# Attention with a mixture of experts: row numbering, routing compares and weight splitting placed on GpSimd, V splitting and softmax denominators placed elsewhere

## The chip, the cores and the metric

The kernel runs on one core of a Trainium2 chip. A core has TensorE (PE in the profile, with its weight loads as PEld), VectorE (DVE), ScalarE (ACT), GpSimd (POOL) and SyncE (SP), each with its own instruction queue that is worked off in order, and DMA queues that SP and POOL feed. The metric is the time of one execution in device microseconds; lower is better. Three executions of the kernel before took 776.6, 773.53 and 778.3 us, so the median is 776.6 us.

## The reference

First attention, then a mixture of experts on its output. Every one of 8 batches and 8 heads has 512 local and 32 global tokens with head dimension 64.

```
s_g  = scale * q_g @ [k_g, k_l]^T          # 32 global queries see everything
out_g = softmax(s_g) @ [v_g, v_l]
s_ll = where(|i - j| <= 32, scale * q_l @ k_l^T, -1e9)
out_l = softmax([scale * q_l @ k_g^T, s_ll]) @ [v_g, v_l]
# softmax: e = exp(s - max); e / (sum(e) + 1e-09)
x = concat([out_g, out_l]) as (4352, 512)

logits = x @ w_gate                        # 8 experts
e_idx  = argmax(logits);  gate_w = softmax(logits)[e_idx]
eom    = sigmoid(x @ w_output_gate)
out[rows of e] = gate_w * eom[e] * (relu(x @ w1[e]) @ w2[e])   # w1 512x1024, w2 1024x512
```

All in float32. Routing is by data: which rows go to which expert is known only when the logits are.

## The kernel before, in words

**Attention.** Per batch there are ten units of work: eight `Local` units (a pair of heads and half of the four 128-query blocks) and two `Global` units (32 queries of four heads each). The list `us` holds four locals, a global, two locals, a global, two locals. `advance(u)` (line 591) makes one step of a pipeline over these units; in step k TensorE computes the scores of unit k (`scores`, into one of two `sp` banks), transposes the probabilities of unit k-2 (`tF`, `tD`, into two `pt` banks), and multiplies unit k-3 with V (`pv`, into one of two `po` banks). In the same step DVE takes the row maximum of unit k (`mx`; for half of the locals, the fused ones, the mask is added in it) and splits the transposed probabilities of unit k-2 into a low half (`loF`, `loD`, lines 309 and 317), each behind the high half that ACT makes (`hiF`, `hiD`, lines 305 and 313); then it normalizes the unit that `pv` finished in the step before: denominators (`den`, L287: sum plus a small constant, times a factor), reciprocal (`rec`, L291), product (`norm`, L340). ACT also makes the exponentials (`ex`, L278). Products run in split float16 or bfloat16, a high and a low half each.

**V.** The V of a batch comes as five float32 tiles `vf` (`load_v`, L131), which `split_v` turns into a float16 half (a copy) and a bfloat16 rest (a subtraction), both on GpSimd; `gp` records each GpSimd call under L83 and keeps their written order. `copy_v` (L141, L142) then copies parts of both halves to other partitions by DMA. For batch 0 all this is written ahead of the first unit, and SP issues the copies ahead of the small constants `ids`, `crt` (L176) and `wrf`.

**Routing.** A `Router` holds four or five tiles of 128 rows (two or three in the last batches). `split` (L439) halves a tile, a DMA transposes it, TensorE makes 16 logits per row. Then `small` gives a list of tiny steps, about twenty, which `fill` slips between the DVE instructions of the attention steps of the next batch: argmax, softmax, a rank of each row among the rows of its expert (`rank`), then `m_fin` (L545: writes the gate into eight columns of each tile, then SP writes the tiles to DRAM, L548) and `m_row` (L538: one 128x128 compare-and-multiply per tile, which marks the place of each row and puts the row's number there). All of these are on DVE. The row numbers `rowf` and a few constants are made by thirteen DVE instructions (L185 to L207) from `crt`; they stand ahead of the first unit's `mx` in DVE's queue. When six batches are routed, `list_pre` (L714) compares the tiles with three early lists (`at_pre`, L717, one DVE instruction) and TensorE gathers the rows of expert 0 that are worked ahead of the others.

**Expert 0's first weights** are loaded in batch 2 (`w1r`, 2 MB). ACT scales and rounds an eighth of them at two places in each of batches 3 to 6 (`ahead1`); the eight low halves (`w1l`, L83) are subtracted on GpSimd in the last batch.

**Order.** The order on PE, DVE, ACT and SP is that in which the program is written (`manual_schedule`); GpSimd's `gp` calls keep theirs too. After attention, at about 340 us, comes the list of all rows and then 36 slots of 128 gathered rows through the experts, which this change does not touch.

Of the kernel before, what the change touches and what calls it, by code (L numbers as in the profile page):

```python
# [10 lines left out]
F32 = mybir.dt.float32  # L11
# [47 lines left out]
def tile_attention_moe(  # L59
# [79 lines left out]
    def copy_v(b):  # L139
        for t in sets[b % 2][0:2]:  # L140
            nc.sync.dma_start(t[0:64, 5:8], t[64:128, 0:3])  # L141
            nc.sync.dma_start(t[64:96, 5:8], t[64:96, 4:5].broadcast_to([32, 3, VW]))  # L142
# [42 lines left out]
    nc.vector.tensor_scalar(rowf, c_k, c_s, 2.0, op0=ALU.add, op1=ALU.add)  # L185
    for n, views in ((4, (rowf[:, 0:16], rowf[:, 17:25])), (2, (rowf[:, 25:33],))):
        far = const.tile([P, 1], F32, name=f"far{n}")
        nc.vector.tensor_scalar(far, c_s, 1.0, n - 1.0, op0=ALU.add, op1=ALU.mult)
        step = const.tile([P, n], F32, name=f"step{n}")
        nc.vector.scalar_tensor_tensor(step, c_k[:, 0:n], -(P - 1.0) / P, far.broadcast_to([P, n]), ALU.mult, ALU.add)  # L190
        for v in views:
            v = v.rearrange("p (b i) -> p b i", i=n)
            nc.vector.tensor_tensor(out=v, in0=v, in1=step.unsqueeze(1).broadcast_to(list(v.shape)), op=ALU.add)
    for r in range(1, 3):
        nc.vector.tensor_scalar(rowf[:, PART[r]:PART[r + 1]], rowf[:, PART[r]:PART[r + 1]], -float(PART[r] * P), None,
                                op0=ALU.add)
# [6 lines left out]
    nc.vector.tensor_copy(count, count_i)  # L203
    slot = const.tile([P, NSLOT + 1], F32, name="slot")
    nc.vector.tensor_scalar(slot, count_i[:, 0:NSLOT + 1], -1.0, None, op0=ALU.add)
    slot_at = const.tile([P, NSLOT + 1], F32, name="slot_at")
    nc.vector.tensor_scalar(slot_at, slot, float(KPRE), float(P), op0=ALU.add, op1=ALU.mult)  # L207

    tile_at = const.tile([P, NT], F32, name="tile_at")
    row_at = const.tile([P, NT, P], F16, name="row_at")  # L210

# [4 lines left out]

    ohsum = const.tile([P, 8], BF16, name="ohsum")
# [373 lines left out]
    def advance(u):  # L591
# [585 lines left out]
```

## Time and profile before

| | us |
|---|---|
| median of three runs | 776.6 |
| the profiled execution's own time | 778.0 |
| its span, first to last instruction | 776.1 |
| PE busy | 692.7 (89%) |
| DVE busy | 399.3 (51%) |
| ACT busy | 362.0 (47%) |
| POOL busy | 211.8 (27%) |
| one batch of attention in the steady part, units 7 to 7 | 34.8 |
| first 20 us: PE busy | 4.5 |

Shares over the whole span say little here, because the program has two parts. Up to about 340 us, attention and routing, PE, DVE and ACT are all busy most of the time; after that the experts run on PE nearly alone. What is asked of a stage has to be read from windows of that stage, and from the chain of waits inside it. Two reading aids: the time of an instruction in the profile includes some overlap with its neighbour on the same engine, so steps are better taken from one start to the next; and a wait for several semaphores is shown under the one that came last.

### The profile page before, as it was taken

To read this page: it belongs to the slowest core of one execution; us is meant where nothing else is said; L and a number is where in the kernel's file an instruction comes from. 1 tells how busy PE (TensorE), PEld (TensorE's weight loads), DVE (VectorE), ACT (ScalarE), POOL (GpSimd) and SP (SyncE) were. 2 spreads that over 40 slices of the span, in tenths; PEclk is the share of its full clock that TensorE was granted. 3 is DMA by queue.
4 is the path that set the end of the run, shared out by engine and by line. 5 is a ranking of instruction groups with operands and counts; after the bars stand their busy time and mean duration, and the time that the engine had idled before them with its cause. 6 is when DMAs were issued, how large, how long until landed. Compare 5 with 4: busy or idle time off the path is not lost.

```text
span 776.1 us, 23116 instructions
## 1 busy us (share of the span) xinstructions
PE 692.7 (89%) x9042; PEld 528.7 (68%) x9042; DVE 399.3 (51%) x1261; ACT 362.0 (47%) x781; POOL 211.8 (27%) x266
## 2 busy tenths in 40 slices
PE   2699999999899987976899989999999978999991
PEld 1588878778676866846677767777776747777760
DVE  0689899898979897770324301133133333332200
ACT  0578777878768787310333411133235151433210
POOL 6333443527241747131011221212221211121110
PEclk9999999999989998997999999999999999999997
DMA  7628696677938466439267594253864959654110
GB/s 225 211 44 240 175 273 185 163 240 144 301 64 272 73 193 140 99 104 314 48 194 248 100 179 104 79 171 78 199 191 142 184 170 189 157 109 89 47 35 21
DMA packets 113604, 120.17 MB, mean 155 GB/s; under 512 B 81551, under 2 KB 83215, under 8 KB 111570
## 3 DMA queue, kind: packets, MB, share of 16 engines
q1 hardware_dynamic: 106706, 96.85, 49.3%
q0 software_dynamic: 6528, 19.67, 8.9%
q14 instruction: 295, 2.42, 1.2%
q8 instruction: 75, 1.23, 0.7%
HBM read 200.50 MB, written 19.42 MB: 283 GB/s over the span
## 4 chain that ended last, share of the span: by engine, by line
issue 45%; PE 19%; DVE 18%; POOL 10%; DMA 2%; ACT 1%; SPq 1%; POOLq 1%; DVEq 0%; ACTq 0%
POOL out_dram L674 5%; POOL qkv L1020 4%; PE sp L249 4%; DVE fl L309 3%; DVE dl L317 3%; DVE p L265 2%; DVE nm L260 2%; PE pt L296 2%; DMA vf<-in_vD_dram 2%; PE pt L301 2%; PE sp L659 1%; DVE row_at L538 1%; POOL qkv L83 1%; PE sp L358 1%; PE pt L387 1%
## 5 line engine op out<-in xcount | busy, mean ns | idle before, releaser
L659 PE MATMUL ph<-qkv,w1h 128*128 128x128 f16 x2304 | 203.7, 222 | 17.4 <-DMA qkv<-qkv 9.8
L659 PEld LDWEIGHTS <-w1h 128*128 128x128 f16 x2496 | 196.9, 100 | 26.7 <-issue 10.5
L659 PE MATMUL ph<-qkv,w1l 128*128 128x128 f16 x1152 | 200.7, 222 | 9.1 <-DVE w1l L686 6.1
L670 PE MATMUL py<-qkv 128*128 128x512 f16 x864 | 192.0, 379 | 0.0
L666 DVE SCALAR_TENSOR_TENSOR qkv<-ph,qkv 128x512 f16<-128x512 f32 x72 | 46.7, 687 | 207.3 <-ACT qkv L665 103.0
L670 PEld LDWEIGHTS <-qkv 128*128 128x128 f16 x896 | 86.0, 98 | 97.0
L659 PEld LDWEIGHTS <-w1l 128*128 128x128 f16 x1248 | 124.2, 100 | 10.3 <-DVE w1l L686 6.4
L665 ACT ACTIVATE qkv<-ph 128x512 f16<-128x512 f32 x72 | 39.8, 594 | 162.4 <-PE ph L659 81.3
L674 POOL DMA_INDIRECT out_dram<-qkv x36 | 36.3, 1008 | 207.6 <-ACT qkv L673 207.0
L249 PE MATMUL sp<-qkv 64*128 64x224 f32 x512 | 69.0, 390 | 20.8 <-DVE nb L265 13.7
L83 POOL TENSOR_TENSOR xr<-xt,xr 128x512 f16<-128x512 f32 x30 | 34.7, 1158 | 152.3 <-ACT xr L439 88.3
L1020 POOL DMA_INDIRECT qkv<-xd,idx x36 | 35.8, 995 | 138.6 <-DMA out_dram<-qkv 135.1
L249 PEld LDWEIGHTS sp<-qkv 64*128 64x128 f32 x512 | 45.7, 194 | 25.0 <-DVE nb L265 14.1
L278 ACT ACTIVATE p<-p,nb 128x224 f32<-128x224 f32 x128 | 51.0, 473 | 24.6 <-DVE nb L265 24.3
L686 DVE SCALAR_TENSOR_TENSOR w1l<-w1r,w1h 128x512 f16<-128x512 f32 x56 | 34.4, 685 | 42.8 <-ACT w1h L684 30.5
L317 DVE SCALAR_TENSOR_TENSOR dl<-pt,dh 128x512 f16<-128x512 f32 x80 | 53.4, 667 | 0.6 <-ACT dh L313 0.2
L690 ACT ACTIVATE qkv<-qkv 128x512 f16<-128x512 f32 x56 | 33.7, 627 | 42.7 <-PE py L670 30.5
L305 ACT ACTIVATE fh<-pt 96x512 f16<-96x512 f32 x64 | 37.7, 589 | 32.9 <-PE pt L296 29.4
L673 ACT ACTIVATE qkv<-py,qkv 128x512 f32<-128x512 f32 x36 | 24.8, 688 | 58.3 <-PE py L670 34.0
L692 DVE SCALAR_TENSOR_TENSOR qkv<-qkv 128x512 f16<-128x512 f32 x56 | 34.5, 686 | 33.3 <-ACT qkv L690 33.3
L313 ACT ACTIVATE dh<-pt 128x512 f16<-128x512 f32 x80 | 47.1, 589 | 8.1 <-PE pt L387 6.0
L328 PE MATMUL po<-qkv,fh 96*128 96x65 f16 x256 | 48.2, 196 | 2.7 <-DVE lg L454 2.7
(189 smaller groups left out, 1473.3 us busy)
## 6 DMA issues: line engine op xcount, KB each, us to landing
w1r<-in_w_dram SPq DMA_DIRECT2D x38, 2048.0 KB
qkv<-in_w_dram SPq DMA_DIRECT2D x38, 2048.0 KB
vf<-in_vD_dram SPq DMA_DIRECT2D x40, 260.0 KB
qkv<-in_kT_dram SPq DMA_DIRECT2D x7, 1280.0 KB
qkv<-in_qT_dram SPq DMA_DIRECT2D x7, 1088.0 KB
xd<-xr SPq DMA_DIRECT2D x6, 1056.0 KB
qkv<-qkv SPq DMA_DIRECT2D x16, 195.0 KB
xd<-xr SPq DMA_DIRECT2D x4, 528.0 KB
```

Source lines behind the costliest of these rows:

```text
L83: i = tc.keep_in_program_order(getattr(nc.gpsimd, name)(*args, **kw))
L249: nc.tensor.matmul(self.sp[:, 2 * hd + bi, 0:W], lhsT=self.q[hs, pr, qs], rhs=self.k[hs, pr, ks], start=(bi == 0 or self.fused), stop=self ...
L278: nc.scalar.activation(self.p[:, n], src, AF.Exp, bias=self.nb[:, n:n + 1], scale=sc)
L313: nc.scalar.mul(self.dh, self.pD, PS)
L317: nc.vector.scalar_tensor_tensor(self.dl, self.pD, PS, self.dh, ALU.mult, ALU.subtract)
L328: nc.tensor.matmul(o, lhsT=fh, rhs=self.vh[0:96, 4 + i, hc], start=True, stop=False)
L659: nc.tensor.matmul(o, lhsT=w[:, k], rhs=xT[:, x], start=(n == 0), stop=(n == 11))
L665: nc.scalar.activation(hh[:, gs], v, AF.Relu)
L666: nc.vector.scalar_tensor_tensor(hl[:, gs], v, 0.0, hh[:, gs], ALU.max, ALU.subtract)
L670: nc.tensor.matmul(py, lhsT=h[:, f], rhs=w, start=(f == 0 and n == 0), stop=(f == 7 and n == 2))
L674: i = nc.gpsimd.indirect_dma_start(out=out[:, :], out_offset=bass.IndirectOffsetOnAxis(ap=x[:, XG:XG + 1].bitcast(U32), axis=0), in_=y, in ...
L1020: nc.gpsimd.indirect_dma_start(out=xs, out_offset=None, in_=xd[:, :], in_offset=bass.IndirectOffsetOnAxis(ap=idx[:, s + 1:s + 2], axis=0))
```

## The change

1. **V of batch 0.** `split_v(0, i)` makes the high half on ACT and the low half on DVE, and is called after the second unit (tiles 0, 4, 1) and after the third (tiles 2, 3). `copy_v` is called in two parts there. The third and fourth head pairs' Q and K are loaded ahead of V's tiles 2 and 3. Batches 1 to 7 keep GpSimd. The load of batch 1's Q and K moves from the first to the third unit of batch 0.
2. **Row numbering.** The thirteen instructions become `number()` on GpSimd, called in the fourth unit of batch 0.
3. **Denominators.** `den` becomes one ACT instruction (`Identity` with a scale and a bias tile `tiny`), and is issued before `mx` in `advance`.
4. **Routing compares.** `m_row` and `m_fin` run on GpSimd, except for the last group.
5. **Early list.** `at_pre` is made by three GpSimd instructions in a step of its own, `list_at`, ahead of `close`; `list_pre` waits at least one step after it.
6. **Expert 0's low halves** are subtracted in batches 4 to 7, two in each.

```diff
 def split_v(b, i):
     vh, vl, _, _ = sets[b % 2]
-    gp.tensor_copy(vh[:, i], raw[i])
-    gp.tensor_sub(vl[:, i], raw[i], vh[:, i])
+    if b == 0:
+        nc.scalar.copy(vh[:, i], raw[i])
+        nc.vector.tensor_sub(vl[:, i], raw[i], vh[:, i])
+    else:
+        gp.tensor_copy(vh[:, i], raw[i])
+        gp.tensor_sub(vl[:, i], raw[i], vh[:, i])
...
-    for i in (0, 4, 1, 2, 3):
+    for i in (0, 4, 1):
         load_v(0, i)
     load_pairs(0, 2, 4)
-    for i in (0, 4, 1, 2, 3):
-        split_v(0, i)
-    copy_v(0)
+    for i in (2, 3):
+        load_v(0, i)
...
-    nc.vector.tensor_scalar(rowf, c_k, c_s, 2.0, op0=ALU.add, op1=ALU.add)
...
+    def number():
+        gp.tensor_scalar(rowf, c_k, c_s, 2.0, op0=ALU.add, op1=ALU.add)
...
 def den(self):
     self.dn = wk.tile([P, 4], F32, name="dn", bufs=4)[self.ps]
-    nc.vector.tensor_scalar(self.dn, self.heads()[:, :, D], PS * 1e-9, 1 / XS, op0=ALU.add, op1=ALU.mult)
+    nc.scalar.activation(self.dn, self.heads()[:, :, D], AF.Identity, bias=tiny[self.ps], scale=1 / XS)
...
 def m_row(t):
     n = self.t0 + t
-    ts(row_at[:, n], count, st["md"][:, t:t + 1], rowf[:, n:n + 1], op0=ALU.is_equal, op1=ALU.mult)
+    (ts if last else gp.tensor_scalar)(row_at[:, n], count, st["md"][:, t:t + 1], rowf[:, n:n + 1], ...)
...
 def m_fin():
     for t in range(T):
-        ts(self.tiles[t][2][:, DM:XG], st["s3"][:, t:t + 1].broadcast_to([P, XG - DM]), YSC, None,
+        (ts if last else gp.tensor_scalar)(self.tiles[t][2][:, DM:XG], ...
...
 # advance
     d = ended.pop(0) if ended else None
+    if d:
+        d[0].den()
     if a:
         a.mx()
         fills(0)
         a.mb()
     if d:
-        d[0].den()
         fills(1)
...
+def list_at():
+    for t in range(KPRE):
+        gp.tensor_scalar(at_pre[:, :, t], tile_at[:, 0:NPRE], float(t * P), None, op0=ALU.is_equal)
+    listed.append(step[0] + 1)
...
 # loop over batches and units
-            if n == 0 and b + 1 < B:
+            if n == (0 if b else 2) and b + 1 < B:
                 load_pairs(b + 1, 0, 4)
...
+            if b == 0 and n in (1, 2):
+                for i in ((0, 4, 1), (2, 3))[n - 1]:
+                    split_v(0, i)
+                copy_v(0, n - 1, 2 * n - 1)
...
+            if b == 0 and n == 3:
+                number()
...
+            if b >= B - 4 and n in (1, 3):
+                f = 2 * (b + 4 - B) + n // 2
+                gp.tensor_sub(w1l[f], w1r[:, :, f * P:(f + 1) * P], w1h[f])
...
-                if n < 8:
-                    gp.tensor_sub(w1l[n], w1r[:, :, n * P:(n + 1) * P], w1h[n])
```

What this does to the order of instructions shows at three places. (The changed file's lines are numbered seven to twenty higher: L131 keeps its number, the copies L141 and L142 become L145 and L146, `mx` L260 and L265 become L267 and L272, `den` L287 becomes L294, the constant `crt` L176 becomes L179.) PE's instructions keep their order throughout.

The first place is SP's queue at the start, from the load of V on. Before:

```order
L131 DMA vf<-in_vD_dram 128x520 x5
L124 DMA qkv<-in_qT_dram 128x1088
L125 DMA qkv<-in_kT_dram 128x2x640
L141 DMA qkv<-qkv 64x1560
L142 DMA qkv<-qkv 32x3x520
```

The changed kernel, at the same place:

```order
L131 DMA vf<-in_vD_dram 128x520 x3
L124 DMA qkv<-in_qT_dram 128x1088
L125 DMA qkv<-in_kT_dram 128x2x640
L131 DMA vf<-in_vD_dram 128x520 x2
L175 DMA ids<-in_c_ids_dram 128x34
L179 DMA crt<-in_c_rt_dram 128x118
L218 DMA wrf<-in_wr_dram 128x4x16
L236 DMA xd<-w1r 1x528
L145 DMA qkv<-qkv 64x520
L146 DMA qkv<-qkv 32x520
```

The copies, which need split V, now stand behind the constants and no longer ahead of them. Before, the rows of `ids` and `crt` follow the copies.

The second place is DVE's queue at the start. Before, the rows between the cast of `identb` and the first `mx` (shown as ISA with its accumulator `nb`) are the numbering; its first two and last three of thirteen:

```order
L152 CAST identb<-ident 128x128
L185 TENSOR_SCALAR rowf<-crt 128x34
L188 TENSOR_SCALAR far_151<-crt 128x1
...
L203 CAST count<-count_i 128x128
L205 TENSOR_SCALAR slot<-count_i 128x42
L207 TENSOR_SCALAR slot_at<-slot 128x42
L265 ISA p,nb<-sp,mask 128x224
```

The changed kernel, at the same place, with the rows up to the first maximum of the fourth unit:

```order
L156 CAST identb<-ident 128x128
L272 ISA p,nb<-sp,mask 128x224
L272 ISA nb 128x1
...
L267 TENSOR_REDUCE nm<-sp 128x4
L138 TENSOR_TENSOR qkv<-vf,qkv 128x520 x3
L267 TENSOR_REDUCE nm<-sp 128x4
L316 SCALAR_TENSOR_TENSOR fl<-pt,fh 96x512
L324 SCALAR_TENSOR_TENSOR dl<-pt,dh 128x512
L138 TENSOR_TENSOR qkv<-vf,qkv 128x520 x2
```

The numbering is gone from the front, and five subtractions of V stand between the first units' work.

The third place is a step in the middle of attention, on ACT and on GpSimd. ACT's rows around the first global unit's exponential (`pgbuf`), before:

```order
L305 ACTIVATE fh<-pt 96x512
L313 ACTIVATE dh<-pt 128x512
L374 ACTIVATE pgbuf_135<-sp,nb 128x544
L305 ACTIVATE fh<-pt 96x512
L313 ACTIVATE dh<-pt 128x512
```

The same rows of the changed kernel:

```order
L312 ACTIVATE fh<-pt 96x512
L320 ACTIVATE dh<-pt 128x512
L294 ACTIVATE dn<-po,tiny 128x4
L381 ACTIVATE pgbuf_121<-sp,nb 128x544
L312 ACTIVATE fh<-pt 96x512
```

A `dn` stands behind each `dh` now, ahead of the exponentials of the step. On GpSimd the rows where a group of four tiles is finished and the next group's split begins, in the changed kernel:

```order
L83 TENSOR_TENSOR qkv<-vf,qkv 128x520
L83 TENSOR_SCALAR xr<-s_1905 128x8 x4
L83 TENSOR_TENSOR xr<-xt,xr 128x512
L83 COPY xr<-ids 128x8
L83 TENSOR_SCALAR row_at<-count,md,rowf 128x128 x4
```

Before, the two rows of TENSOR_SCALAR aren't there, and the rows of `xr` follow the last of V directly.

More of the change, by code (lines that the diff above doesn't have):

```diff
@@ L184, in tile_attention_moe @@
     rowf = const.tile([P, NT], F32, name="rowf")
[L185 to L196, printed above, removed]
     part = const.tile([P, 3], F32, name="part")
@@ L202, in tile_attention_moe @@
     count = const.tile([P, P], BF16, name="count")
-    nc.vector.tensor_copy(count, count_i)
     slot = const.tile([P, NSLOT + 1], F32, name="slot")
-    nc.vector.tensor_scalar(slot, count_i[:, 0:NSLOT + 1], -1.0, None, op0=ALU.add)
     slot_at = const.tile([P, NSLOT + 1], F32, name="slot_at")
-    nc.vector.tensor_scalar(slot_at, slot, float(KPRE), float(P), op0=ALU.add, op1=ALU.mult)
     tile_at = const.tile([P, NT], F32, name="tile_at")
     row_at = const.tile([P, NT, P], F16, name="row_at")
+    def number():
+        gp.tensor_scalar(rowf, c_k, c_s, 2.0, op0=ALU.add, op1=ALU.add)
+        for n, views in ((4, (rowf[:, 0:16], rowf[:, 17:25])), (2, (rowf[:, 25:33],))):
+            far = const.tile([P, 1], F32, name=f"far{n}")
+            gp.tensor_scalar(far, c_s, 1.0, n - 1.0, op0=ALU.add, op1=ALU.mult)
+            step = const.tile([P, n], F32, name=f"step{n}")
+            gp.tensor_scalar(step, c_k[:, 0:n], -(P - 1.0) / P, far, op0=ALU.mult, op1=ALU.add)
+            for v in views:
+                v = v.rearrange("p (b i) -> p b i", i=n)
+                gp.tensor_tensor(out=v, in0=v, in1=step.unsqueeze(1).broadcast_to(list(v.shape)), op=ALU.add)
+        for r in range(1, 3):
+            gp.tensor_scalar(rowf[:, PART[r]:PART[r + 1]], rowf[:, PART[r]:PART[r + 1]], -float(PART[r] * P), None,
+                                    op0=ALU.add)
+        gp.tensor_copy(count, count_i)
+        gp.tensor_scalar(slot, count_i[:, 0:NSLOT + 1], -1.0, None, op0=ALU.add)
+        gp.tensor_scalar(slot_at, slot, float(KPRE), float(P), op0=ALU.add, op1=ALU.mult)
     wrf = const.tile([P, 4, 16], F32, name="wrf")
@@ L215, in tile_attention_moe @@
     wrh, wrl = wrhl[:, :, 0:16], wrhl[:, :, 16:32]
+    tiny = const.tile([P, 1], F32, name="tiny")
+    nc.gpsimd.memset(tiny, PS * 1e-9 / XS)
     ohsum = const.tile([P, 8], BF16, name="ohsum")
@@ L537, in m_row @@
                 n = self.t0 + t
-                ts(row_at[:, n], count, st["md"][:, t:t + 1], rowf[:, n:n + 1], op0=ALU.is_equal, op1=ALU.mult)
+                (ts if last else gp.tensor_scalar)(row_at[:, n], count, st["md"][:, t:t + 1], rowf[:, n:n + 1], op0=ALU.is_equal, op1=ALU.mult)
             def m_s3():
@@ L544, in m_fin @@
                 for t in range(T):
-                    ts(self.tiles[t][2][:, DM:XG], st["s3"][:, t:t + 1].broadcast_to([P, XG - DM]), YSC, None,
+                    (ts if last else gp.tensor_scalar)(self.tiles[t][2][:, DM:XG], st["s3"][:, t:t + 1].broadcast_to([P, XG - DM]), YSC, None,
                        op0=ALU.mult)
@@ L712, in tile_attention_moe @@
     ixp = const.tile([P, KPRE], U32, name="ixp")
-    def list_pre():
-        at = const.tile([P, NPRE, KPRE], F16, name="at_pre")
-        shape = list(at.shape)
-        nc.vector.tensor_tensor(out=at, in0=tile_at[:, 0:NPRE].unsqueeze(2).broadcast_to(shape),
-                                in1=c_k[:, 0:KPRE].unsqueeze(1).broadcast_to(shape), op=ALU.is_equal)
-        rows_of(ixp, scratch(), at, NPRE, const.tile([P, 2, KPRE], F32, name="tmp_pre"))
+    at_pre = const.tile([P, NPRE, KPRE], F16, name="at_pre")
+    listed = []
+    def list_at():
+        for t in range(KPRE):
+            gp.tensor_scalar(at_pre[:, :, t], tile_at[:, 0:NPRE], float(t * P), None, op0=ALU.is_equal)
+        listed.append(step[0] + 1)
+    def list_pre():
+        rows_of(ixp, scratch(), at_pre, NPRE, const.tile([P, 2, KPRE], F32, name="tmp_pre"))
     def fetch_pre():
```

11 lines of the change are left out of this document (6 added, 5 removed).

## The prediction

> **What bounds the kernel now.** I read the busy times by window first, then the chain of waits, then the timeline where the chain changes engine. From about 340 us on, the experts run on PE nearly alone; the change has nothing there. So the question is attention, up to 340 us, and the chain of work that ended last shows its beat: the second global unit of each batch starts at these times (two more, at 178.06 and 251.18, are bounds of the windows below)
>
> ```profile
> 42.77 0.99 PE sp L358 x8
> 73.48 0.99 PE sp L358 x8
> 108.31 0.99 PE sp L358 x8
> 143.16 0.99 PE sp L358 x8
> 214.14 1.86 PE sp L358 x8
> ```
>
> Between these starts (the last window ends where the eighth batch's second global unit begins), the windows give span, then busy time and instructions of PE, PEld, DVE, ACT and POOL:
>
> ```profile
> 42.77:73.48 30.71, 30.71 (x519) 26.14 (x522) 27.46 (x93) 25.34 (x63) 7.98 (x11) 1.00 0.64 170
> 73.48:108.31 34.83, 32.87 (x539) 26.63 (x543) 31.89 (x123) 26.30 (x64) 14.40 (x20) 1.00 0.74 234
> 143.16:178.06 34.90, 32.87 (x540) 26.62 (x543) 32.05 (x124) 28.46 (x68) 13.79 (x19) 1.00 0.67 186
> 178.06:214.14 36.08, 33.14 (x548) 27.71 (x552) 32.98 (x125) 28.66 (x69) 17.59 (x24) 0.97 0.78 210
> 214.14:251.18 37.04, 35.08 (x539) 27.84 (x543) 32.72 (x125) 28.58 (x68) 11.28 (x16) 0.94 0.57 167
> 251.18:286.70 35.52, 32.98 (x536) 26.61 (x536) 32.59 (x125) 28.28 (x68) 19.52 (x24) 1.00 0.57 143
> ```
>
> This is the best evidence in the trace. The first interval has the same ten units but no small routing steps, and PE is busy all of its 30.71 us. From the second on DVE does some thirty more instructions (4.4 us), PE only a few logits and ranks more, and the interval is 4.1 us longer while PE falls idle for 2 us: DVE's added work is paid nearly one for one. So a router batch is bound by DVE in its routing half, and by PE in the rest.
>
> The start has a bound of its own:
>
> ```profile
> 18.34 0.63 SPq L142 DMA_DIRECT2D qkv<-qkv  x1
> 19.64 0.46 SPq L176 DMA_DIRECT2D crt<-in_c_rt_dram  x1
> 22.02 0.24 DVE L185 TENSOR_SCALAR rowf<-crt 128x34 f32<-128x34 f32 x1 [19.15 <-DMA crt<-in_c_rt_dram]
> 25.32 1.87 PE L249 MATMUL sp<-qkv 64*128 64x224 f32 x8 [13.71 <-DVE nb L265]
> 34.44 0.64 PE L296 MATMUL pt<-ident,p 128*96 128x128 f32 x4
> ```
>
> DVE's first thirteen instructions number the rows; they wait for `crt`, which SP issues behind the copies of V, which wait for GpSimd's split. So the third unit's scores, which need a bank that the first `mx` frees, stand still for 13.7 us while everything they need but `mx` is there.
>
> **The start.** With the numbering on GpSimd and `crt` ahead of the copies, the first `mx` has only its scores and the mask to wait for. What is late next is data, or V. These two rows show the second unit's scores, which waited for K, and its mask product; below them the DMA engines' load and rate in 40 slices of the first 45 us, 1.125 us each:
>
> ```profile
> 8.99 1.86 PE L249 MATMUL sp<-qkv 64*128 64x224 f32 x8 [2.61 <-DMA qkv<-in_kT_dram]
> 10.79 0.82 PE L254 MATMUL sp<-mask,identb 128*128 128x128 bf16 x4
> ...
> GB/s 0 62 336 306 168 286 311 399 413 423 396 305 113 4 0 94 205 189 117 113 147 418 369 401 416 407 398 396 296 6 15 0 0 0 0 7 0 0 15 0
> ```
>
> The first burst is over after 13 slices, at about 14 us; the last two V tiles (520 KB, 1.3 us at 400 GB/s) now stand behind the third and fourth pair, so that pair is there at about 12.6 us. The third unit's scores move from 25.3 to 12.6: 12.7 us is the most that the start can give. Then V is late: five casts on ACT and five subtractions on DVE stand in the first units' way. Their nearest rows, with those that the rest of the sum needs (line, shapes, count, total us, mean ns, idle before):
>
> ```profile
> L439 ACT CAST xr<-xt 128x512 f16<-128x512 f32 x32 | 19.4, 608 | 0.0
> L440 DVE TENSOR_TENSOR xr<-xt,xr 128x512 f16<-128x512 f32 x2 | 1.3, 688 | 0.0
> L287 DVE TENSOR_SCALAR dn<-po 128x4 f32<-128x4 f32 x64 | 9.7, 152 | 0.0
> L271 ACT ACTIVATE nb<-nm 128x4 f32<-128x4 f32 x32 | 6.4, 201 | 3.2 <-DVE nm L260 2.8
> L391 ACT ACTIVATE fh<-pt 96x128 f16<-96x128 f32 x16 | 4.3, 270 | 0.5 <-PE pt L382 0.5
> L538 DVE TENSOR_SCALAR row_at<-count,md,rowf 128x128 f16<-128x128 bf16 x34 | 14.1, 443 | 0.0
> L83 POOL COPY xr<-ids 128x8 int32<-128x8 int32 x32 | 6.0, 189 | 0.0
> L201 POOL IOTA count_i<- 128x128 int32 x1 | 0.2, 235 | 0.0
> masks.py:199 POOL TENSOR_SCALAR_AFFINE_SELECT ident<-ident 128x128 f32<-128x128 f32 x1 | 0.3, 336 | 0.1
> ```
>
> Walked through: the second unit's mask product ends at 11.6, its maximum at 12.7, its exponentials at 14.6, three casts at 16.2, the three subtractions (each behind its cast) at 17.1. The maximum of the third unit ends at 18.1 and its exponentials at 20; the last two casts come at 21, their subtractions at 22, and only then the fourth unit's maximum (23) and the second unit's first low half. So the third unit's first transpose, at 34.44 before, comes at 23.7: 10.7 us. The first four DMA copies of V are issued by 18.3 and land about 2 us later, inside this. I take **10.5 us**. If casts and subtractions covered nothing of each other, they would be 5 x 0.61 + 5 x 0.69 = 6.5 us of the 12.7: bounds 6.2 and 12.7. The numbering's thirteen instructions on GpSimd lie where it now has nothing else to do.
>
> **The routing half of a batch.** The chain through one of them (start, length on the chain):
>
> ```profile
> 94.08 0.07 DVE dn L287
> 99.74 0.39 DVE xr L545 x4
> 102.11 0.30 DVE row_at L538
> 103.01 0.62 DVE row_at L538
> 104.06 0.22 DVE row_at L538
> ```
>
> Off the chain go `row_at` (0.06 for the first, then 0.30, 0.62 and 0.22: 1.2 us), `m_fin` (0.39) and six or seven `dn` (0.07 where they overlap a neighbour, 0.15 to 0.19 where they don't: 0.6): 2.2 us per interval, 13.2 in the six router intervals. That is the price if nothing new binds. From the other end: PE's need is 30.71 plus two logits of 0.30 and a rank of 0.3, 31.6 us; with 0.6 for places where another engine still ends last, 32.2, and 0.5 more in the four intervals where ACT also scales weights. The six now take 34.83 + 34.85 + 34.90 + 36.08 + 37.04 + 35.52 = 213.2 us and would take 2 x 32.2 + 4 x 32.7 = 195.2: 18 us less. This includes the 5 us by which three of them exceed 34.85: in the fifth the PE stood still around 209 us, and then ran at half speed (the 1.86 in the first fence, against 0.99).
>
> ```profile
> 209.85 1.34 DVE L538 TENSOR_SCALAR row_at<-count,md,rowf 128x128 f16<-128x128 bf16 x2
> 209.98 1.17 POOL L83 TENSOR_TENSOR xr<-xt,xr 128x512 f16<-128x512 f32 x1 [3.44 <-ACT xr L439]
> L538 DVE TENSOR_SCALAR row_at<-count,md,rowf x34: 279/306/1145, 101.9 to 336.2; 128x128 f16<-128x128 bf16 x34
> ```
>
> There two `row_at` ended when a GpSimd subtraction ended (minimum, median and maximum of one `row_at` are 279, 306 and 1145 ns). I take **14 us**, near the chain's own sum, since ACT will not let PE reach its need. The first interval is PE's already: nothing.
>
> The Trainium skill, Advanced Engine Details and Errata, section VectorE Performance Modes, says that VectorE shares one of its memory ports with GpSimd, and that GpSimd instructions and VectorE's two-port modes block each other. The trace agrees: 1145 ns against 306. The rule speaks against the change, since GpSimd gets more to do; by it the sum is that of the fourth rival below.
>
> **ACT** gets 80 `dn`. Its rows lie between 201 ns (the same 128x4, from SBUF) and 270 ns (a PSUM source, 128 wide); I take 0.22: 2.2 us per interval, on 26.3 to 28.7 busy of 34.8, so 28.5 to 30.9 of 32.5. It waits for nothing: the `pv` it reads ended a step earlier. Behind it wait the exponentials, with a step of slack, and DVE's `rec`, which comes after the low half that waits for the same high halves. Its cover is PE's step of 3.2 us; where ACT also casts and scales weights (two or three steps a batch) that cover is gone, and 0.2 us per such step is lost, the 0.5 above. By ScalarE: Activation LUTs, section Rules for kernel authors, in the Trainium skill, an instruction with a bias tile costs about 0.3 us; by it four intervals would lose some 0.4 us each more, and the sum would be 1.6 us less. No row here has this shape.
>
> **GpSimd** gets per interval four `row_at` (0.24 to 0.34 by the rows of IOTA and AFFINE_SELECT, one input of 128x128; 0.3 taken) and four gates (0.19): 2 us on 14 of 34.8. The queue behind them holds the next tile's split, with its transpose and, four steps later, its logit; SP's write of the tiles now waits for GpSimd, and batch V loads and transposes stand behind it on SP. With GpSimd idle 14 us before that point, none is late by a step. Expert 0's low halves move to where GpSimd idles too, and its last batch gets emptier.
>
> **The end of attention**: `at_pre` (0.25), two `row_at` (0.9) and a few `dn` leave the chain: 1.5 us, between 0 and 3.
>
> Sum: 10.5 + 14 + 1.5 = **26 us**. The profiled execution took 778.0 us (span 776.1), 1.4 above the median; 778.0 - 26 = 752.0, and for the median 776.6 - 26 = 750.6, so **751 us**.
>
> **The rivals.**
> 1. Only the start gains, because ACT takes DVE's place: at 28.5 + 2.2 to 2.7 it is busier than DVE would be. For it: ACT was busy without a break where weights are scaled. Against: its exponentials have a step of slack. Attention then gives up to 5 us: 776.6 - 10.5 - 3.5 = 763.
> 2. The start gains little, because V is split between the first units: 5 us instead of 10.5, 756.5. For it: casts wait behind exponentials. Against: half the time now lost is a wait with no work in it.
> 3. Slower: GpSimd becomes the bound of a batch. Its queue has 34.85 - 14 = 20.9 us free for eight new instructions, so it decides from 2.6 us each. At 4 us a batch would take 46 us, six of them 67 us more, and even with the start's gain 776.6 + 67 - 10.5 = 833; already at 3.2 us it is 794. Against: no GpSimd row of this size passes 0.34 us.
> 4. GpSimd's added time holds up DVE's other two-input steps. Such a step (L524) took 0.91 us under a GpSimd subtraction and 0.15 on the mean of five others; one more per interval is 0.8 x 6 = 4.8 us: 755.5.
>
> ```profile
> 205.24 1.17 POOL L83 TENSOR_TENSOR xr<-xt,xr 128x512 f16<-128x512 f32 x1 [12.27 <-ACT xr L439]
> 205.52 0.91 DVE L524 SCALAR_TENSOR_TENSOR s<-eg,s 128x5 f32<-128x5 f32 x1
> ...
> L524 DVE SCALAR_TENSOR_TENSOR s<-eg,s 128x4 f32<-128x4 f32 x5 | 0.7, 146 | 0.0
> ```
>
> That the change doesn't do what it says is out: the order shows each instruction on its new engine.
>
> **How the numbers follow.** Forecast 0.57; rival 1 0.20, rival 2 0.08, rival 4 0.08, rival 3 0.03; 0.04 that gains of both stages stay under 8 us. Unknown costs reach from 12.7 + 18 + 3 = 34 us of gain (743) to 6.2 + 5 = 11 us (765): the range is 743 to 765. A measurement tells about 1% (7.8 us) from no change. Faster by more: 0.91 (the forecast, 1, 2 and 4, less a little); within: 0.06; slower by more: 0.03 (rival 3).
>
> **What would show it.** Right: the third unit's scores before 14 us and its first transpose before 25 (34.44 before); router intervals of 32 to 33 us with PE busy over 97% of them, DVE under 29; no `dn` on DVE; PE not at half speed after the fifth interval. Wrong: intervals of 34 with ACT busy over 32 (rival 1); third scores early but the fourth and fifth units waiting for DVE's subtractions (rival 2); GpSimd's `row_at` over 2 us (rival 3); DVE's tiny steps at 0.9 us in most batches (rival 4). An experts' part that differs by over 2 us would be something I have no reason for.

## The result and the profile after

| | before | changed |
|---|---|---|
| median of four runs, us | 777.45 (773.53 to 778.62) | 747.9 (746.35 to 749.27) |
| ratio, 95% interval | | 0.963 (0.959 to 0.967) |
| profiled execution, us | 778.0 | 746.95 |
| its span, us | 776.1 | 745.1 |

The change is 29.6 us faster by the medians, 31.0 us between the two profiled executions. The forecast was 26 us (751, range 743 to 765).

First the windows again, cut at the same events as before: from the start of one batch's second global unit to the next (span, then busy time and instructions of PE, PEld, DVE, ACT and POOL, granted clock, DMA share, GB/s). The changed kernel:

```profile
32.33:63.03 30.70, 30.70 (x519) 26.08 (x522) 27.25 (x83) 26.60 (x73) 11.88 (x16) 1.00 0.64 171
63.03:95.56 32.53, 32.31 (x539) 26.42 (x543) 29.48 (x105) 27.99 (x77) 17.42 (x27) 1.00 0.73 211
95.56:128.11 32.55, 32.33 (x539) 26.40 (x543) 29.64 (x105) 28.50 (x76) 17.85 (x27) 1.00 0.79 227
128.11:160.68 32.57, 32.34 (x539) 26.43 (x543) 29.65 (x105) 29.90 (x79) 20.01 (x29) 1.00 0.73 204
160.68:194.09 33.41, 32.22 (x548) 26.77 (x552) 30.18 (x106) 30.20 (x82) 20.09 (x30) 1.00 0.81 225
194.09:226.62 32.53, 32.31 (x539) 26.43 (x543) 29.59 (x105) 29.64 (x78) 22.19 (x32) 1.00 0.73 188
226.62:259.35 32.73, 32.51 (x538) 26.47 (x538) 29.67 (x107) 29.23 (x77) 20.22 (x30) 1.00 0.74 178
```

Two things are to be seen. The first window begins at 32.33 where it began at 42.77: 10.44 us were gained ahead of it. And the six router intervals, 34.83 to 37.04 before, are 32.53 to 33.41 now, with PE busy 99% of five of them and at full clock in all. The first interval is what it was, 30.70.

The end of attention is read from the step on DVE that lists all rows, here before and in the changed kernel:

```profile
339.74 1.61 DVE L944 TENSOR_TENSOR qkv<-tile_at,sl_at 128x1394 f16<-128x1394 f32 x1
```

```profile
310.65 1.61 DVE L964 TENSOR_TENSOR qkv<-tile_at,sl_at 128x1394 f16<-128x1394 f32 x1
```

So the 31.0 us of the two profiles divide like this:

| step | forecast | measured | how |
|---|---|---|---|
| start | 10.5 | 10.4 | 42.77 - 32.33 |
| six router intervals | 14 | 16.9 | 213.2 - 196.3 |
| end of attention | 1.5 | 1.7 | (339.74 - 286.70) - (310.65 - 259.35) |
| experts | 0 | 1.9 | (776.1 - 339.74) - (745.1 - 310.65) |

The last row is scatter: the experts' part of the very same changed kernel took 434.5 us in this profile and 437.9 us in another one. From here on attention is read from its stages, which repeat far better.

The moved instructions, by line and shapes, in attention of the changed kernel (count, total us, mean ns, idle before):

```profile
L83 POOL TENSOR_SCALAR row_at<-count,md,rowf 128x128 f16<-128x128 bf16 x31 | 24.5, 802 | 1.1 <-DVE md L538 1.1
L294 ACT ACTIVATE dn<-po,tiny 128x4 f32<-128x4 f32 x64 | 16.4, 257 | 0.0
```

A `row_at` takes GpSimd 0.80 us, not the 0.24 to 0.34 of the estimate, and a `dn` takes ACT 0.26 us, not 0.22. Neither shows in the intervals; why not, and where it would, is what two of the experiments ask.

### The profile page after: what moved, and what is told of

The parts are those of the page before. It is cut to its first block, busy times and chain, and to the rows that moved or that the text cites. A ratio compares the mean times of both kernels' runs of the same rounds, so it can differ in the third digit from the quotient of the medians.

```text
span 745.1 us, 23135 instructions
## 1 busy us (share of the span) xinstructions
PE 686.4 (92%) x9042; PEld 525.4 (71%) x9042; DVE 379.4 (51%) x1110; ACT 377.3 (51%) x866; POOL 240.4 (32%) x335
## 3 DMA queue, kind: packets, MB, share of 16 engines
q1 hardware_dynamic: 106898, 96.85, 51.2%
## 4 chain that ended last, share of the span: by engine, by line
issue 47%; PE 27%; POOL 10%; DVE 8%; ACT 4%; DMA 1%; SPq 1%; POOLq 1%; DVEq 0%; ACTq 0%
PE sp L256 6%; POOL out_dram L683 5%; POOL qkv L1040 4%; PE pt L303 3%; PE pt L308 3%; PE sp L365 2%; DVE dl L324 2%; PE sp L668 1%; DMA qkv<-in_kT_dram 1%; DVE nm L267 1%; PE pt L394 1%; DVE fl L316 1%; PE sp L261 1%; PE po L421 1%; ACT qkv L709 1%
## 5 line engine op out<-in xcount | busy, mean ns | idle before, releaser
L668 PEld LDWEIGHTS <-w1h 128*128 128x128 f16 x2496 | 197.0, 100 | 24.0 <-issue 10.5
L272 DVE CUSTOM_DVE_ANT_0 p<-sp,mask 128x224 f32<-128x224 f32 x128 | 42.2, 385 | 15.3 <-PE sp L256 6.2
```

The costliest lines, as they stand in the source:

```text
L272: nc.vector.tensor_tensor_reduce(self.p[:, n], self.sp[:, n, 0:W], mask[:, self.half + n % 2], -0.125, 3e38, ALU.add, ALU.min, self.nb[:, ...
L668: nc.tensor.matmul(o, lhsT=w[:, k], rhs=xT[:, x], start=(n == 0), stop=(n == 11))
```

## The experiments

The theory behind the forecast: the start was lost to DVE's wait for a constant, and in the routing half DVE's instructions are paid one for one. The rivals: ACT, or GpSimd, takes DVE's place; V is late at the start; or, since DVE idles nearly 3 us in each interval now, PE is the bound and some of what was moved need not have been.

All stages in one table, for each kernel's profile, so that the texts below can be short. "Start" is the first matmul of batch 0's second global unit (0.07 us ahead of the row that the chain and the windows above use), the intervals run from there by the same unit, "end" is from the last of them to the step that lists all rows. The ratios are to the kernel before, run beside each on the same chip; four kernels ran once, so they have a single time and no ratio. The times come from several chips, so the stages compare better than the last column.

| kernel | start | six router intervals | their sum | end | us, ratio (95%) |
|---|---|---|---|---|---|
| before | 42.70 | 34.83 34.85 34.90 36.08 37.04 35.59 | 213.3 | 53.0 | |
| changed | 32.26 | 32.53 32.55 32.57 33.41 32.53 32.79 | 196.4 | 51.3 | 747.9, 0.963 (0.959 to 0.967) |
| changed, again | 33.49 | 32.54 32.77 32.57 33.42 32.53 32.79 | 196.6 | 51.3 | 748.1, 0.968 (0.966 to 0.971) |
| start_only | 31.89 | 34.83 34.85 34.88 36.15 35.41 35.57 | 211.7 | 50.8 | 759.3, 0.987 (0.982 to 0.992) |
| crt_first | 38.05 | 34.83 34.86 34.89 35.32 37.97 35.58 | 213.5 | 52.3 | 769.0, 0.997 (0.994 to 1.001) |
| v_pool | 30.15 | 32.53 32.54 32.57 33.40 32.52 32.78 | 196.3 | 51.3 | 742.0, 0.963 (0.958 to 0.969) |
| den_dve | 32.48 | 33.09 33.13 33.16 33.38 33.10 33.45 | 199.3 | 49.3 | 747.3, 0.974 (0.968 to 0.980) |
| rows_dve | 31.97 | 34.25 34.28 34.28 35.74 37.03 34.40 | 210.0 | 51.7 | 760.6, 0.989 (0.985 to 0.992) |
| rows_four | 33.31 | 32.53 35.03 38.17 38.95 43.50 40.22 | 228.4 | 62.1 | 785.7, one run |
| tail_back | 32.16 | 32.52 32.55 32.57 33.41 32.52 33.58 | 197.2 | 59.7 | 755.8, one run |
| w1l_back | 32.63 | 32.52 32.56 32.56 33.42 32.53 33.59 | 197.2 | 54.5 | 746.6, one run |
| list_back | 33.35 | 32.53 32.77 32.57 33.41 32.54 32.78 | 196.6 | 54.3 | 754.1, one run |
| lists_pool3 | 29.95 | 32.23 32.41 32.44 33.14 32.40 32.50 | 195.1 | 51.7 | 745.4, 0.962 (0.955 to 0.968) |
| best | 26.50 | 32.23 32.43 32.44 33.13 32.40 32.51 | 195.1 | 51.7 | 737.3, 0.955 (0.951 to 0.959) |

The table has its own measure of noise: the start of kernels whose code is the same up to there lies between 32.0 and 33.5 us, the intervals agree within 0.03 us but for the second router interval, which is 32.55 or 32.77. The experts' part, the span less all that stands ahead of it, is 429 to 438 us. Where the texts below number the intervals, the one of 30.70 us ahead of the six is the first, as in the prediction.

**start_only** is the kernel before with edits 1 and 2 alone.

```diff
+        if b == 0:
+            nc.scalar.copy(vh[:, i], raw[i])
+            nc.vector.tensor_sub(vl[:, i], raw[i], vh[:, i])
...
+            if b == 0 and n == 3:
+                number()
```

> The kernel before with only the start changed: V of batch 0 split on ScalarE and VectorE, the small constants issued ahead of the copies of V, the row numbering on GpSimd. Theory (the gains of the start and of the routing half stand apart): the second global unit of batch 0 starts at 32.3 us as in the changed kernel (42.77 before), the router intervals stay at 34.8 to 37 us, and the time is 10.4 us below the kernel before. Rival (the start's gain needs the denominators off VectorE too): the second global unit starts at 34 us or later and the time is at most 8 us below.

The start is at 31.9 us, the intervals are those of before, and the time is 8.5 us (1.3%) below. The two gains stand apart, as the sum had it.

**crt_first** is the kernel before with one block moved.

```diff
     load_pairs(0, 2, 4)
+    ids = const.tile([P, NT], I32, name="ids")
+    nc.sync.dma_start(ids, c_ids)
+    crt = const.tile([P, 80 + RPE + 4], F32, name="crt")
+    nc.sync.dma_start(crt, c_rt)
     for i in (0, 4, 1, 2, 3):
         split_v(0, i)
     copy_v(0)
```

> The kernel before with one thing changed: SyncE issues the loads of ids and crt ahead of the copies of V (the numbering stays on VectorE ahead of the first maximum, V is split on GpSimd ahead of the first unit). Theory (the start was lost to the place of this one load behind the copies): the numbering no longer waits for crt but for the list that GpSimd makes between its subtractions at 16.3 us, the first maximum starts at about 17 us (23.93 before), the second global unit of batch 0 at about 36 us (42.77 before), and the time is about 7 us below the kernel before, two thirds of the changed kernel's gain at the start. Rival (the numbering must leave VectorE, or V is late anyway): the second global unit at 40 us or later.

Neither number came: the start is 38.05 us, 4.65 us earlier than before. Two things stood between, both in DVE's rows:

```profile
15.49 0.80 DVE L185 TENSOR_SCALAR rowf<-crt 128x34 f32<-128x34 f32 x1 [12.62 <-DMA crt<-in_c_rt_dram]
...
16.52 1.63 DVE L193 TENSOR_TENSOR rowf<-rowf,step 128x16 f32<-128x16 f32 x2
...
18.24 1.24 DVE L190 SCALAR_TENSOR_TENSOR step<-crt,far 128x2 f32<-128x2 f32 x1
...
20.36 0.39 DVE L265 CUSTOM_DVE_ANT_0 p<-sp,mask 128x224 f32<-128x224 f32 x1
```

`crt`, issued at 9.4 us, is there only at 15.5, behind the loads that were issued ahead of it. And the numbering now runs beside GpSimd's split of V: the pair of additions takes 1.63 us where it took 0.25 in the kernel before, the step 1.24 where it took 0.16. So the place of the load in SP's queue is 4.65 of the 10.4 us (starts scatter by 1.5 us, and the whole time, 0.997, is not clear of noise). The rest came when the numbering left DVE's queue and V's split went behind the first units; no run takes these two apart.

**v_pool** is the changed kernel with V of batch 0 split on GpSimd again, at the new place.

```diff
-        if b == 0:
-            nc.scalar.copy(vh[:, i], raw[i])
-            nc.vector.tensor_sub(vl[:, i], raw[i], vh[:, i])
-        else:
-            gp.tensor_copy(vh[:, i], raw[i])
-            gp.tensor_sub(vl[:, i], raw[i], vh[:, i])
+        gp.tensor_copy(vh[:, i], raw[i])
+        gp.tensor_sub(vl[:, i], raw[i], vh[:, i])
```

> The changed kernel with V of batch 0 split on GpSimd, at the same place of the program, so that its split no longer stands in front of the numbering's constants or of the first maximum; the rest as changed. Theory (what cost the start was the wait of VectorE for the constants, and not where V is split): the casts and subtractions leave ScalarE and VectorE, GpSimd starts at about 9.6 us and ends at about 19 us, and the third unit's first transpose comes 1 to 3 us before its 23.55 us: 1 to 3 us faster than the changed kernel. Rival (V is what the first units wait for once the constants are early): the first product with V comes after 21 us (19.89 in the changed kernel) and the time is 1 us or more slower.

The theory: the start comes at 30.15 us, 2.1 to 3.3 us ahead of the changed kernel's two profiles, although the third unit's first transpose is only 0.7 us earlier (22.85); the whole times (0.963 against 0.963 and 0.968) do not separate the two kernels. By the stage, this part of edit 1 costs time; what gained was to take the split and the copies out of the way of `crt` and of the first `mx`. The new bound is data, as the third unit's scores show (they wait for K, and run at half speed after the wait; three units later such a row takes 1.03 us):

```profile
14.36 1.86 PE L252 MATMUL sp<-qkv 64*128 64x224 f32 x8 [2.44 <-DMA qkv<-in_kT_dram]
...
24.59 1.03 PE L252 MATMUL sp<-qkv 64*128 64x224 f32 x8
```

**den_dve** has the denominators back on DVE at their old place, `tiny` taken out.

```diff
-            nc.scalar.activation(self.dn, self.heads()[:, :, D], AF.Identity, bias=tiny[self.ps], scale=1 / XS)
+            nc.vector.tensor_scalar(self.dn, self.heads()[:, :, D], PS * 1e-9, 1 / XS, op0=ALU.add, op1=ALU.mult)
```

> The changed kernel with the denominators back on VectorE at their old place, the rest as changed. Theory (VectorE's instructions are paid one for one in the routing half): 0.6 us more in each of six router intervals, so 33.1 us each and 3.6 us more in all than the changed kernel. Rival (TensorE bounds the intervals now, with 2.9 us of VectorE's time unused in each): intervals stay at 32.5 us and the time is the changed kernel's within 1 us. Second rival (ScalarE's extra 1.5 us per interval holds something up): faster than the changed kernel.

Its windows of the second to fourth batch:

```profile
63.19:96.28 33.09, 32.37 (x538) 26.57 (x535) 30.18 (x114) 26.09 (x65) 17.31 (x27) 1.00 0.73 224
96.28:129.41 33.13, 32.39 (x539) 26.59 (x536) 30.30 (x116) 26.95 (x67) 17.88 (x27) 1.00 0.77 206
```

One for one, as the theory has it: 0.56 to 0.66 us in five of the six intervals and nothing in the five-tile one (33.38 us), 2.9 in all, although DVE idles 2.9 us there. The share of busy time misleads: PE idles 0.7 us in these windows and 0.2 in the changed kernel's, so DVE must be the bound for some steps of an interval and PE for the others. But the whole gains next to nothing: the end of attention is 2.0 us shorter with the denominators on DVE (49.3 against 51.3), so edit 3 is worth about 1 us of the 31. Why ACT's `dn` costs 2 us there was not tried.

**rows_dve** has `m_row` and `m_fin` back on DVE.

```diff
-                (ts if last else gp.tensor_scalar)(row_at[:, n], count, ...)
+                ts(row_at[:, n], count, ...)
...
-                    (ts if last else gp.tensor_scalar)(self.tiles[t][2][:, DM:XG], ...)
+                    ts(self.tiles[t][2][:, DM:XG], ...)
```

> The changed kernel with the compares of each tile's rows and the gates back on VectorE, the rest as changed. Theory (one for one): 1.6 us more in each of six router intervals, 34.1 us each, 9.6 us in all; and if these compares beside GpSimd's subtractions are what made the fifth to seventh intervals longer before, those come out 1 to 2 us above the others again, 12 us in all. Rival (TensorE bounds with slack): under 5 us in all, intervals under 33.3 us.

Four intervals are 1.6 to 1.7 us longer (the chain's rows had given 1.6), the fifth 2.3 and the sixth 4.5: 13.6 us in all. Two of the three long ones that the expectation named came; the seventh is 34.40 us, like the others. PE's waits around the five-tile group, with the compares on DVE and then in the changed kernel:

```profile
PE pt L394 <- DVE dl L324: 1.7, 1, 1.7
PE po L335 <- DVE s L548: 0.8, 1, 0.8
PE pt L389 <- DVE fl L316: 0.5, 1, 0.5
```

```profile
PE po L335 <- DVE s L548: 0.8, 1, 0.8
PE pt L394 <- DVE dl L324: 0.4, 1, 0.4
```

And what made `dl` late, on DVE and on GpSimd at that moment of rows_dve:

```profile
197.35 1.34 DVE L545 TENSOR_SCALAR row_at<-count,md,rowf 128x128 f16<-128x128 bf16 x2
199.87 1.33 DVE L545 TENSOR_SCALAR row_at<-count,md,rowf 128x128 f16<-128x128 bf16 x2
```

```profile
197.47 1.17 POOL L83 TENSOR_TENSOR xr<-xt,xr 128x512 f16<-128x512 f32 x1 [3.44 <-ACT xr L446]
...
199.42 1.17 POOL L83 TENSOR_TENSOR qkv<-vf,qkv 128x520 bf16<-128x520 f32 x1
```

```profile
201.22:238.25 37.03, 35.49 (x538) 28.19 (x536) 32.29 (x114) 30.42 (x78) 13.81 (x18) 0.92 0.56 168
```

The first pair of compares ends within 0.05 us of GpSimd's subtraction, the second lies under the next one; PE stands still for 1.7 us, and the sixth interval then has a granted clock of 0.92, with PE busy 35.5 us on the work that takes it 32.3 in the changed kernel. So 3.2 of its 4.5 us are slower products.

**rows_four** writes each of GpSimd's compares four times.

```diff
+                for _ in range(1 if last else 4):
                     (ts if last else gp.tensor_scalar)(row_at[:, n], count, ...)
```

> The changed kernel with each of GpSimd's row compares written four times, so 3.2 us for each tile where there were 0.8; the result is the same. Theory (GpSimd has 10 to 15 us of idle time in each interval, and nothing in the next four steps waits for a compare): the intervals stay within 0.3 us of 32.53, 32.55 and 32.57 up to the fourth batch, and the sixth, where GpSimd is busiest, is at most 2 us longer. Rival (the splits queued behind the compares come late and the logits with them; by the prediction's count a compare of over 2.6 us decides): every interval 3 us or more longer, over 15 us in all.

The theory falls and the rival holds in the main: 32 us more in the six intervals, 38 us more in the time, though the first router interval loses nothing and the second 2.5 us. From the fourth interval on a part is a lower granted clock (0.96 down to 0.84, PE busy 35.5 us in the sixth for 32.3). GpSimd is not full, only 27.3 of 35.0 us busy in the first interval that suffers:

```profile
96.54:131.57 35.03, 32.47 (x538) 26.62 (x535) 30.67 (x105) 28.27 (x76) 27.26 (x39) 1.00 0.69 186
208.69:252.19 43.50, 35.47 (x538) 28.94 (x536) 31.29 (x106) 29.96 (x78) 35.44 (x49) 0.84 0.57 148
```

It is the order of its queue. The compares of a group stand in one block ahead of the next tile's split, and behind that of V of the next batch:

```profile
128.44 13.87 POOL L83 TENSOR_SCALAR row_at<-count,md,rowf 128x128 f16<-128x128 bf16 x16
142.28 1.16 POOL L83 TENSOR_TENSOR xr<-xt,xr 128x512 f16<-128x512 f32 x1
```

so PE waits for the transposed tile and for copies of V (three rows of its waits from 96.5 to 209 us), and DVE for the buffer `xt` (PE waits another 2.7 us for that `xt` in turn):

```profile
PE po L458 <- DMA xT<-xr: 3.3, 3, 2.3
...
PE po L336 <- DMA qkv<-qkv: 1.6, 1, 1.6
PE po L335 <- DMA qkv<-qkv: 0.7, 1, 0.7
```

```profile
DVE xt L347 <- POOL xr L83: 3.4, 3, 1.4
```

**tail_back**, **w1l_back** and **list_back** undo edits 5 and 6, together and apart.

```diff
-            if b >= B - 4 and n in (1, 3):
-                f = 2 * (b + 4 - B) + n // 2
-                gp.tensor_sub(w1l[f], w1r[:, :, f * P:(f + 1) * P], w1h[f])
...
             if b == B - 1:
+                if n < 8:
+                    gp.tensor_sub(w1l[n], w1r[:, :, n * P:(n + 1) * P], w1h[n])
```

```diff
 def list_pre():
-    rows_of(ixp, scratch(), at_pre, ...)
+    at = const.tile([P, NPRE, KPRE], F16, name="at_pre")
+    ...
+    nc.vector.tensor_tensor(out=at, ..., op=ALU.is_equal)
+    rows_of(ixp, scratch(), at, ...)
...
-    smalls.extend((r, f) for f in (list_at, close, list_pre, fetch_pre))
+    smalls.extend((r, f) for f in (close, list_pre, fetch_pre))
```

> The changed kernel with the early list compared on VectorE again and expert 0's low halves all subtracted in the last batch again. Theory (both only touch the end of attention): the intervals up to the sixth stay within 0.1 us, the stretch from the last batch's second global unit to the step that lists all rows grows by 0 to 1.5 us from its 51.3 us. Rival (the low halves spread over batches 4 to 7 cost something in those intervals): the third to sixth router intervals come out shorter than 32.57, 33.41, 32.53 and 32.79 us by 0.3 us or more.

This was far out: the end grows by 8.4 us and the last interval by 0.8. The other five intervals stay within 0.02 us, so the rival falls too. Two more runs took the edits apart.

> The changed kernel with only expert 0's low halves back in the last batch, one in each of eight steps. Theory A (these subtractions push GpSimd's last row compares back, and TensorE waits for those rows when it makes the early list): most of the 8 us that the end of attention lost with both edits undone is lost here too. Theory B (the early list on VectorE lost it): 1 us or less is lost here.

> The changed kernel with only the early list's compare back on VectorE, in the same step in which TensorE makes the list. Theory A (GpSimd's late row compares lost the time): 2 us or less is lost here, since the last compare ends 2 us earlier without the extra subtractions. Theory B (the list's own place, without a step of its own after the last compare): TensorE waits 3 us or more for the list here and the end of attention is 5 us or more longer.

Neither theory alone: the low halves cost 3.2 us at the end and 0.8 in the last interval, the list 3.0 us, both together 9.2. (The single time of w1l_back, 746.6 us, does not show its 4 us, since its experts' part, 430 us, was among the shortest.) PE's longest wait at the end of attention in tail_back, w1l_back and list_back, in this order:

```profile
PE po L571 <- DVE at_pre L725: 5.5, 1, 5.5
```

```profile
PE pt L303 <- DVE fl L402: 2.6, 1, 2.6
```

```profile
PE po L571 <- DVE at_pre L725: 1.3, 1, 1.3
```

In list_back the list stands in DVE's queue behind the rest of its step: GpSimd's last row compares are over at 260.34, the list begins at 262.83. In tail_back it begins at 262.19, also behind the last compares (260.82), but then lasts 4.43 us instead of 0.23. The list in tail_back and in list_back:

```profile
262.19 4.43 DVE L725 TENSOR_TENSOR at_pre<-tile_at,crt 128x75 f16<-128x75 f32 x1
```

```profile
262.83 0.23 DVE L725 TENSOR_TENSOR at_pre<-tile_at,crt 128x75 f16<-128x75 f32 x1
```

and GpSimd in tail_back, the first and the last of four subtractions in a row:

```profile
262.04 1.15 POOL L83 TENSOR_TENSOR w1l<-w1r,w1h 128x512 f16<-128x512 f32 x1
...
265.37 1.15 POOL L83 TENSOR_TENSOR qkv<-qkv 128x512 f16<-128x512 f32 x1
```

The list ends at 266.62 us, the last subtraction at 266.52. So it was not late compares, as theory A had it, but one small step of DVE held up by GpSimd's subtractions, of which two are low halves that edit 6 had moved away. A lower clock came on top: in the 8 us behind that wait the granted clock is 0.60, and PE is busy 51.2 us at the end of tail_back and 48.8 of list_back, against 47.4 in the changed kernel.

With the low halves alone the same thing happens to other steps. DVE is busy 39.48 us at the end of w1l_back and 35.50 us in the changed kernel, with 158 instructions in each:

```profile
260.51:314.99 54.48, 47.65 (x724) 37.65 (x722) 39.48 (x158) 29.33 (x70) 29.56 (x42) 0.97 0.53 111
```

```profile
259.34:310.65 51.31, 47.38 (x724) 37.57 (x722) 35.50 (x158) 29.20 (x70) 25.15 (x36) 0.97 0.54 118
```

```profile
265.54 2.28 DVE L482 TENSOR_TENSOR dl<-lg,m 128x16 f32<-128x16 f32 x1
274.15 2.13 DVE L516 TENSOR_TENSOR ohsum<-ohsum,os 128x8 bf16<-128x8 bf16 x1
```

```profile
265.50 1.18 POOL L83 TENSOR_TENSOR w1l<-w1r,w1h 128x512 f16<-128x512 f32 x1
266.61 1.18 POOL L83 TENSOR_TENSOR qkv<-qkv 128x512 f16<-128x512 f32 x1
```

Two steps that take 0.16 to 0.17 us elsewhere last until a second GpSimd subtraction ends (267.79 and 276.25 us). This is rival 4's mechanism, and edits 5 and 6 are what keep it small here.

**lists_pool3** is v_pool with three more small steps on GpSimd.

```diff
-                nc.vector.tensor_copy(new("md", [P, T]), st["mi"])
+                (nc.vector if last else gp).tensor_copy(new("md", [P, T]), st["mi"])
...
-                tt(out=tile_at[:, self.t0:self.t0 + T], ...)
+                (tt if last else gp.tensor_tensor)(out=tile_at[:, self.t0:self.t0 + T], ...)
...
-                tt(out=ohsum, in0=ohsum, in1=st["os"], op=ALU.add)
+                (tt if last else gp.tensor_tensor)(out=ohsum, in0=ohsum, in1=st["os"], op=ALU.add)
```

> The changed kernel with V of batch 0 split on GpSimd and three more of VectorE's small steps per batch on GpSimd (the cast that gives the place of a row, the subtraction that gives its tile, the running count of rows), the last group excepted. Theory (VectorE is still the bound in the routing half although it idles 2.9 us per interval): 0.2 to 0.35 us less in each of six intervals, 32.2 to 32.35 us, 1.2 to 2 us in all, beside the 2.1 us of the start. Rival (TensorE is the bound now): intervals stay at 32.5 us.

Between the two: 0.12 to 0.3 us per interval, 1.3 in all. What DVE can still give in the routing half is nearly used up: in five of the six intervals PE idles only 0.1 to 0.2 us. They are still 0.6 to 0.9 us above the 31.6 that the prediction counted as PE's need, and nearly all of that lies in PE's own busy time (32.0 to 32.4 us), where the profile names no wait; why stays open.

**best** is lists_pool3 with one load moved.

```diff
     load_pairs(0, 1, 2)
+    load_pairs(0, 2, 3)
     for i in (0, 4, 1):
         load_v(0, i)
-    load_pairs(0, 2, 4)
+    load_pairs(0, 3, 4)
```

> The version with V of batch 0 split on GpSimd and three more small steps on GpSimd, and with the third head pair's Q and K loaded ahead of V's first tiles. Theory (data is what the third unit's scores wait for once V is off ScalarE and VectorE): those scores start at about 11.5 us (14.36 with V on GpSimd, 14.05 in the changed kernel), the second global unit of batch 0 at 28 to 29 us (30.15), and the whole is 4 to 6 us below the changed kernel. Rival (V, now 1.5 us later, is waited for instead): the second global unit stays at 30 us, 3 us or less below the changed kernel.

> The changed kernel once more, beside the next three on the same chip. Both theories: its own stage times again (second global unit of batch 0 at 32.3 us, intervals of 32.53 us), and 0.96 to 0.965 of the kernel before.

The third unit's scores come right behind the second unit's:

```profile
8.69 1.87 PE L253 MATMUL sp<-qkv 64*128 64x224 f32 x8 [2.24 <-DMA qkv<-in_kT_dram]
10.49 0.82 PE L258 MATMUL sp<-mask,identb 128*128 128x128 bf16 x4
11.24 1.49 PE L253 MATMUL sp<-qkv 64*128 64x224 f32 x8
```

and the start is 26.5 us, 3.5 us ahead of lists_pool3 and more than expected. Beside the changed kernel on the same chip it takes 737.3 us against 748.1; the stages up to the list of all rows account for 8 of these 11 us, the rest lies in the scatter of the experts' part. It beats both kernels.

## Why the prediction was right

**The bound.** Right. DVE was paid one for one in the routing half (den_dve 0.56 to 0.66 us in five of six intervals where the chain gave 0.6, rows_dve 1.6 to 1.7 where it gave 1.6), and the first interval, PE's own, did not move. One of the prediction's signs was missed: DVE is busy 29.5 to 30.2 us in the router intervals, and under 29 was named.

**The start.** Right in size, 10.4 for 10.5, and in its path. The third unit's scores start at 14.05 us where the walk had 12.6 and the sign named was "before 14"; this cost nothing, since their maximum stood behind DVE's subtractions of V until 16.8 us anyway, and the first transpose came at 23.55 for 23.7. To hit within 0.1 us is luck all the same, since the start of this very code scatters by 1.5 us. The walk counted V's casts and subtractions as what is late; v_pool shows that this was the change's own doing, 2 to 3 us of the possible gain and so rival 2 in small, and crt_first that 4.65 us of the gain lie in the order of SP's queue alone.

**The routing half.** The mis-sized term: 14 us forecast, 16.9 measured. The step that failed is "since ACT will not let PE reach its need": ACT scales weights twice in the intervals of 32.57 and 32.53 us (and in the five-tile one), once in that of 32.55, and not at all in the one of 32.53, so the 0.5 us put down to ACT there is nothing, and its `dn` of 0.26 us show no price there either. By the chain's own sum, 13.2, what was missing are the long intervals: 2.3 us in each of the six make 13.8, and 3.1 us more came because the three long ones moved nearer to the others. They were counted only in the floor of 18 us; rows_dve shows that they hang on the moved compares themselves: 6.8 of its 13.6 us are in the fifth and sixth. How long they are is in part a matter of where the compares fall: with the routing of before, the sixth is 37.04, 35.41 and 37.97 us in before, start_only and crt_first.

**GpSimd.** The cost of nothing was right, the price was not: 0.80 us for a `row_at`. Its cover, 14 us of idle time, was also measured by the wrong thing. rows_four shows that a block of compares may hold up the queue although GpSimd idles 8 us in the same interval. At 3.2 us for each of eight instructions rival 3 put the time at 794. The run, with four or five compares of that length in most intervals, gave 785.7, but by this other way: what it added to GpSimd stayed below the 20.9 us of free time by which the point of 2.6 us was worked out.

**The end.** 1.7 for 1.5 is right by accident. The kernel before and start_only have the same instructions there, and take 53.0 and 50.8 us, at granted clocks of 0.94 and 1.00:

```profile
286.70:339.74 53.04, 47.68 (x724) 38.40 (x722) 39.69 (x180) 26.81 (x60) 20.27 (x23) 0.94 0.49 113
```

```profile
274.28:325.04 50.76, 45.62 (x724) 36.33 (x722) 41.05 (x180) 26.84 (x60) 20.30 (x23) 1.00 0.50 118
```

So 1.7 us is no more than such a spell at a lower clock. Of the edits, the denominators on ACT cost 2.0 us there by the one profile of den_dve, and edits 5 and 6, which the sum gave 0.25 us and nothing, keep 9 us from being lost. start_only has neither of them and loses nothing, its list takes 0.31 us; whether edits 3 and 4 made them needed, or only the moment at which the list falls, is not shown.

**Rival 4** did not come as priced, but was near: in the changed kernel one such row is left in the fifth interval (`s`, 0.98 us) and one in the end (`pb`, 0.81 us), and w1l_back and tail_back show the size that it can have: 2.3 and 4.4 us in one step.

## What to carry to other kernels

An engine with idle time can still be paid one for one: ask which stretch of a period each engine decides, and test it by putting one small thing back. What is moved to an idle engine costs what its queue holds up, so look at the length of the block and what stands behind it, not at the free share. Look, too, for small steps that take many times their usual length in one place (here 4.43 us for 0.23): they name a neighbour that holds them up. When work leaves an engine at the start, ask whether the one that it came from is not now the better place for something else: of six edits here one half of the first was best left undone.

## What the runs showed of the hardware

GpSimd takes 0.80 us for the compare-and-multiply of 128x128 that takes DVE 0.31 us in the median. The Trainium skill, GPSIMD Engine Reference, section 4.1 Engine selection, calls GpSimd's one-input operations roughly line-rate; its cast of 128x520 (0.62 us, and ACT's 0.65) fits that. This compare, with one tile as input beside two values per partition, does not: 128 elements per partition take it longer than the cast takes for 520.

DVE and GpSimd hold each other up, and both ways. In crt_first DVE's step of 0.16 us took 1.24 us beside GpSimd's subtractions. In the changed kernel GpSimd's first numbering instruction took 1.33 us while DVE subtracted V, and in v_pool, with V on GpSimd itself, 0.44 us:

```profile
15.76 1.33 POOL L83 TENSOR_SCALAR rowf<-crt 128x34 f32<-128x34 f32 x1 [11.02 <-DMA crt<-in_c_rt_dram]
```

```profile
19.12 0.44 POOL L83 TENSOR_SCALAR rowf<-crt 128x34 f32<-128x34 f32 x1
```

The Trainium skill, SBUF — State Buffer, section Who interferes with whom, says that a VectorE instruction with two inputs in SBUF contends with a GpSimd instruction that reads SBUF, and that the port pair which they share is an exclusive lock. The runs agree: `dl` and `ohsum` in w1l_back and `at_pre` in tail_back are such instructions, and the first of them ended at 267.82 us, GpSimd's second subtraction at 267.79. They add that DVE's step does not get in between GpSimd's instructions: it was held through two of them there, and through four in tail_back.
